# Two-layer linear attention and MLP on one core: the deferred queries' min(q, 0) on VectorE, and layer 0's tiles 6 and 7 turned by VectorE

## The chip, the cores and the metric

The kernel runs on one core of a Trainium2 chip, in one launch. The metric is the device time of that core in microseconds (us). Before the change it is 867.03 us, the median of 3 runs (866.54 to 867.05).

The engines of a core have one instruction stream each and run at the same time: TensorE (PE in the profile; its weight loads are listed apart as PEld), VectorE (DVE), ScalarE (ACT), GpSimd (POOL) and SyncE (SP). They wait for each other through semaphores. Within one engine the instructions run in the order in which they were written. Here SP issues nearly all DMA transfers, one after the other, and an issue whose data is not yet there holds all issues behind it.

## The reference

Two layers, each an attention block and then an MLP block, over x of 2048 rows by 448. Cut to what matters here:

```python
phi = lambda t: jnp.where(t > 0, t + 1, jnp.exp(t)) + 1e-6
pq, pk = phi(q), phi(k)                      # q, k, v from layernorm(x) @ wqkv, 16 heads of 28
kv = jnp.einsum("bhsd,bhse->bhde", pk, v)
z = jnp.einsum("bhsd->bhd", pk)
num = jnp.einsum("bhqd,bhde->bhqe", pq, kv)
den = jnp.einsum("bhqd,bhd->bhq", pq, z)[..., None] + 1e-6
x = x + (num / den).transpose(...).reshape(B, S, D) @ wo
x = x + gelu(layernorm(x) @ w1 + b1) @ w2 + b2
```

The kernel computes phi as max(t, 0) + exp(min(t, 0)), with the 1e-6 added elsewhere. Everything is in float32; each matmul operand is split into a high and a low part, and three products of these parts make up one float32 product.

## The kernel before

x is handled in 16 row tiles of 128 (0 to 15), four to a block. Each layer has three stages.

Phase 1 (`phase1`) makes, for each tile t, the keys K(t), the queries Q(t) of tiles up to 8, and G, the running sum of x'k that later gives kv; G of tile t - 1 follows K(t) on TensorE. For K and Q the normalised tile is needed transposed, as `XH` (high part) and `XL` (low part). There are two ways to get there. For tiles below `TURNED[l]` (8 in layer 0, 0 in layer 1) TensorE transposes four pieces into a PSUM bank `tp` (`stage_b`, line 264), and ScalarE and VectorE split the bank into XH and XL (lines 276 and 277); the 64-column tail of such a tile is first copied twice by ScalarE (line 446). For the others VectorE turns 32x32 blocks into a tile `sq` (`turn`, lines 303 and 304), SP stores two turned tiles together to DRAM (`store_sq`, line 310) and reads them back spread over the partitions in four transfers (`spread`, line 318), and ScalarE and VectorE split the spread tile `sp` (`split_t`, lines 335 and 336).

The order of the work in a step t of phase 1 is written out as a string of tokens, `STEP`, with exceptions in `STEPS`: K, G and Q are the products; T the TensorE transposes of tile t + 1; X the split of tile t + 1 into XH and XL; s the split of tile t for G; kp, kh and kl the key's phi and its parts; a and n the normalisation of a later tile (`a10` is tile 10), tu or v its turn, sp the spread; qp the previous query's phi and its store to DRAM; bg a piece of the weights' loading and splitting; ld a load of x. In a product, `k_at`, `q_at` and `g_at` say at which places the low parts stand among the high ones.

The last products of phase 1 and the transition to the MLP are ordered by the tokens of `ORDER`: Q, Qy and Qa are products of the deferred queries of tiles 9 to 15; T3 and x3 the TensorE transposes and split of the last tile of the first MLP block, sp0 and sp1 the spreads of its first three tiles (half of these eight transfers are issued by ScalarE), x0 to x2 their splits; Qi is `phi_first` (ScalarE's relu(-q) and exp of its negative, lines 579 and 580), Qj `phi_last` (VectorE's max and sum, line 585, and SP's store), pre four loads of stored queries. After the last token ScalarE loads the table for Gelu and the first MLP product `hp` is issued.

The MLP stage runs over four blocks of four tiles, with 14 column groups each: `mlp1` makes `hp` for one group ahead (11 matmuls), ScalarE its Gelu `g` and high part `gh` (lines 974 and 977), VectorE its low part `gl` (line 978), and `mlp2` the 12 matmuls into `y` (lines 1001 to 1003: gh by w2h, gh by w2l, gl by w2h, for four tiles).

Of the kernel before, what the change touches and what calls it, by code (L numbers as in the profile page):

```python
# [11 lines left out]
AF = mybir.ActivationFunctionType  # L12
OP = mybir.AluOpType
# [9 lines left out]
def linear_attn_mlp_kernel(  # L23
# [12 lines left out]
    pe, act, dve, pool, sp = nc.tensor, nc.scalar, nc.vector, nc.gpsimd, nc.sync  # L36
    x0 = x_in[0]
    y_out = out[0]
    S, D = x0.shape
    F = w1.shape[1]  # L40
    H, DH = 16, 28
    NT = S // 128
    NB = NT // 4
    NF = F // 128
    G = 112
# [27 lines left out]
    def t512(tag, bufs, name, dt=F32, at=0):  # L73
        n = 576 if tag in "BF" else 512
        return work.tile([128, n], dt, name=name, tag=tag, bufs=bufs)[:, at:at + 512]
# [339 lines left out]
    bg = bg_pieces()  # L415
# [14 lines left out]
    sts = {}  # L430


    TURNED = (8, 0)
    tails = {}

    def stage_a(l, t):
# [46 lines left out]

    def k_at(l, t):
        if t < 9:
            return (3, 6, 9, 11) if t == 0 or l == 0 and 2 < t < 8 else (2, 5, 8, 11)
        return (2, 5, 8, 11) if t == 9 else (1, 4, 7, 10)

    def q_at(l, t):
        if t < 9:  # L490
            return (2, 5, 8, 11) if l == 0 and t < 7 else (2, 4, 7, 10) if t == 0 else (1, 4, 7, 10)
        return {11: (4, 7, 10, 11), 12: (5, 7, 9, 11),
                13: (5, 8, 10, 11), 15: (1, 5, 8, 11)}.get(t, (1, 4, 7, 10))

    def g_at(l, t):
        if t < 9:
            return (4, 7, 10) if l == 0 and 0 < t < 6 else (3, 6, 9)
        return (2, 5, 8) if t < NT - 1 else (2, 6, 9)

    def stage_k(l, t, cs=range(4)):  # L500
# [44 lines left out]
    qo = []  # L545
# [3 lines left out]
    def stage_q(l, t, cs=range(4), tag=None):  # L549
        if tag:  # L550
            qs_[l, t] = bank(tag, 4, "psq")[:, :D]
        qs_[l, t] = proj("q", ("a", l, t // 4), t % 4, qs_.get((l, t)), cs, q_at(l, t))
        if 3 in cs:
            qo.append((l, t, qs_.pop((l, t))))
# [19 lines left out]
    begun = []  # L574

    def phi_first():
        l, t, o = qo.pop(0)
        e = t512("e" if t < NT - 2 else "E", 3 if t < NT - 2 else 2, "eq")[:, :D]
        act.activation(e, o, AF.Relu, scale=-1.0)
        act.activation(e, e, AF.Exp, scale=-1.0)  # L580
        begun.append((l, t, o, e))

    def phi_last():
        l, t, o, e = begun.pop(0)
        dve.scalar_tensor_tensor(e, o, 0.0, e, op0=OP.max, op1=OP.add)
        sp.dma_start(pq_d[l][t * 128:(t + 1) * 128, :], e)
# [21 lines left out]
    def stage_g(l, t, acc, mid=lambda: None):  # L608
# [22 lines left out]
    ORDER = [  # L631
# [4 lines left out]
    ] * LAYERS  # L636
    DEFER = NT - sum(tok in ("Q", "Qa", "Qy") for tok in ORDER[0].split())

# [1 line left out]
    STEPS = {  # L640
# [9 lines left out]
    }  # L650
    NORM = (
# [464 lines left out]
    for l in range(LAYERS):  # L1116
# [11 lines left out]
        def pre(j):  # L1128
# [4 lines left out]

        tok_ = SimpleNamespace(
            Q=lambda j: stage_q(l, fill.pop(0)), Qp=lambda j: fill_qphi(), Qv=lambda j: stage_qphi(j or 9),
            Qi=lambda j: phi_first(), Qj=lambda j: phi_last(), Qx=lambda j: stage_q(l, fill[0], (0,)),
            Qy=lambda j: stage_q(l, fill.pop(0), (1, 2, 3)),
            Qa=lambda j: stage_q(l, fill.pop(0), tag="acc"), G=lambda j: stage_g(l, NT - 1, acc, lambda: trans_z(tr, zs[l])),
            ld=lambda j: (load_pq(l, 0, j), load_x(l, j)), gt=lambda j: trans_gt(tr, acc),
# [77 lines left out]
```

## Time and profile before

| | |
|---|---|
| median of 3 runs | 867.03 us |
| the profiled execution | 866.77 us |
| its span, first to last instruction | 865.0 us |
| granted TensorE clock | 1.00 throughout |
| data moved by DMA | 95.81 MB, mean 111 GB/s |
| DVE, ACT and POOL busy | 57%, 41% and 24% of the span |

Times in the profile's rows are microseconds from the start of the span. A row of a timeline has the start, the duration, the engine, the line of the kernel, the operation, what it writes and reads, and in brackets the idle time before it with what ended it. TensorE pipelines its matmuls: a row's duration is longer than the distance to the next, so its rate is read from starts or from windows. SPq and ACTq are DMA issues. A window's row has its length, the busy time and count of each engine, the granted clock, the DMA engines' share and GB/s.

### The profile page before, as it was taken

Reading aid. Unit: us, or ns where it says so; the run is one execution under the profiler, and the core shown is the slowest. Engines: PE = TensorE matmul, PEld = TensorE weight load, DVE = VectorE, ACT = ScalarE, POOL = GpSimd, SP = SyncE. Lnnn points to the kernel's source line nnn. Section 1 sums busy time; section 2 is a strip of 40 time slices with the busy share of each in tenths; the row PEclk is TensorE's granted clock in tenths of the full one; section 3 lists DMA queues with packets and bytes.
Section 4 is the critical chain, followed back from the end, with each engine's and each line's share of the span. In section 5 each row is a group of like instructions: output and inputs, shape, how many; then the busy total and the mean of one; then the engine's idle time right before and its main releaser. Section 6 shows DMA issues by size and latency. Waiting matters only on the chain.

```text
span 865.0 us, 11671 instructions
## 1 busy us (share of the span) xinstructions
PE 859.5 (99%) x4173; PEld 769.9 (89%) x4173; DVE 489.9 (57%) x956; ACT 354.0 (41%) x634; POOL 209.1 (24%) x242
## 2 busy tenths in 40 slices
PE   9999999999999999999999999999999999999998
PEld 8999988888888888888899998988888888888887
DVE  7888676559455443236477877664674383533112
ACT  6776656333323322333356565632232233223231
POOL 3565612235013012012222343120220140140000
PEclk9999999999999999999999999999999999999999
DMA  5475546633313502051145543362332423111001
GB/s 168 131 241 178 187 112 206 194 112 109 135 60 114 150 0 98 1 182 49 49 149 187 164 129 97 108 217 81 116 107 91 135 74 114 50 49 42 1 1 43
DMA packets 65082, 95.81 MB, mean 111 GB/s; under 512 B 9088, under 2 KB 59904, under 8 KB 65024
## 3 DMA queue, kind: packets, MB, share of 16 engines
q1 hardware_dynamic: 63696, 94.13, 33.8%
q10 hardware_dynamic: 1328, 0.93, 0.4%
q8 instruction: 33, 0.54, 0.3%
q14 instruction: 25, 0.20, 0.1%
HBM read 56.70 MB, written 35.13 MB: 106 GB/s over the span
## 4 chain that ended last, share of the span: by engine, by line
PE 95%; ACT 2%; DMA 1%; DVE 1%; issue 0%; POOL 0%; ACTq 0%; SPq 0%; DVEq 0%
PE hp L972 31%; PE y L1002 10%; PE y L1001 10%; PE y L1003 10%; PE G L622 8%; PE psk L353 8%; PE psq L353 5%; PE op L891 2%; PE op L890 2%; PE op L892 2%; DMA sp<-sq_m 1%; PE op L880 1%; PE op L879 1%; PE op L881 1%; PE kvp L786 1%; PE mp L796 1%
## 5 line engine op out<-in xcount | busy, mean ns | idle before, releaser
L978 DVE TENSOR_TENSOR gl<-g,gh 128x512 fp32r<-128x512 f32 x112 | 83.2, 743 | 293.2 <-ACT gh L977 293.2
L974 ACT ACTIVATE g<-hp,b1s 128x512 f32<-128x512 f32 x112 | 77.1, 688 | 400.1 <-PE hp L972 400.1
L1002 PE MATMUL y<-w2l,gh 128*128 128x448 f32 x447 | 163.6, 366 | 0.0
L1001 PE MATMUL y<-w2h,gh 128*128 128x448 f32 x447 | 162.2, 363 | 0.0
L1003 PE MATMUL y<-w2h,gl 128*128 128x448 f32 x447 | 160.3, 359 | 0.1
L972 PE MATMUL hp<-XH,w1h 128*128 128x512 f32 x336 | 130.7, 389 | 0.0
L972 PE MATMUL hp<-XH,w1l 128*128 128x512 f32 x336 | 130.7, 389 | 0.0
L972 PE MATMUL hp<-XL,w1h 128*128 128x512 f32 x336 | 130.1, 389 | 0.0
L215 POOL TENSOR_TENSOR brs<-bve,mhalf 128x1 f32<-128x1 f32 x55 | 34.8, 632 | 258.4 <-DVE bve L214 257.9
L1001 PEld LDWEIGHTS y<-w2h,gh 128*128 128x128 f32 x447 | 83.7, 187 | 9.8 <-ACT gh L977 0.5
L1002 PEld LDWEIGHTS y<-w2l,gh 128*128 128x128 f32 x447 | 83.9, 188 | 6.9
L1003 PEld LDWEIGHTS y<-w2h,gl 128*128 128x128 f32 x447 | 84.0, 188 | 5.8 <-DVE gl L978 0.9
L972 PEld LDWEIGHTS hp<-XL,w1h 128*128 128x128 f32 x336 | 63.1, 188 | 13.1
L972 PEld LDWEIGHTS hp<-XH,w1h 128*128 128x128 f32 x336 | 63.0, 187 | 10.7
L972 PEld LDWEIGHTS hp<-XH,w1l 128*128 128x128 f32 x336 | 63.1, 188 | 9.9
L977 ACT CAST gh<-g 128x512 fp32r<-128x512 f32 x112 | 69.6, 622 | 3.6
L840 POOL TENSOR_TENSOR pz<-pq,zb 128x448 f32<-128x448 f32 x32 | 37.0, 1162 | 103.3 <-DVE dn L846 67.1
L353 PE MATMUL psk<-wk,XH 128*128 128x448 f32 x210 | 61.8, 364 | 0.0
L353 PE MATMUL psq<-wq,XH 128*128 128x448 f32 x196 | 57.5, 366 | 0.0
L478 POOL TENSOR_TENSOR xnl<-x,xnh 128x384 fp32r<-128x384 f32 x32 | 35.0, 1092 | 69.3 <-ACT xnh L477 56.0
L622 PE MATMUL G<-kh,xnh 128*128 128x448 f32 x128 | 46.8, 368 | 0.0
L336 DVE TENSOR_TENSOR XL<-sp,XH 128x512 fp32r<-128x512 f32 x54 | 45.3, 851 | 2.1 <-ACT XH L335 2.1
(185 smaller groups left out, 1491.1 us busy)
## 6 DMA issues: line engine op xcount, KB each, us to landing
x<-in_A_x_dram SPq DMA_DIRECT2D x32, 224.0 KB, 3.7
pq_d<-eq SPq DMA_DIRECT2D x32, 224.0 KB, 2.7
pq<-pq_d SPq DMA_DIRECT2D x32, 224.0 KB, 3.1
sq_m<-sq SPq DMA_DIRECT2D x14, 512.0 KB, 2.6
x<-x_d SPq DMA_DIRECT2D x32, 224.0 KB, 3.7
sp<-sq_m SPq DMA_DIRECT2D x52, 128.0 KB, 2.8
sq_a<-sq SPq DMA_DIRECT2D x12, 512.0 KB, 2.9
sp<-sq_a SPq DMA_DIRECT2D x48, 128.0 KB, 2.7
```

Source lines behind the costliest of these rows:

```text
L336: eng.tensor_tensor(lo.rearrange("p (c i n) -> p c i n", c=4, n=32), x, f(h), op=OP.subtract)
L353: pe.matmul(o, x, p, start=(i == 0), stop=(i == 10))
L478: pool.tensor_tensor(lo[:, :TL], xn[:, :TL], f(h[:, :TL]), op=OP.subtract)
L622: pe.matmul(acc[c], w, k, start=first and c not in others[0], stop=last and c not in others[1])
L840: pool.tensor_tensor(pz, pqt[l, b * 4 + j], tr.zb, op=OP.mult)
L972: pe.matmul(o, w, r, start=(k == 0), stop=(k == len(made) - 1))
L974: act.activation(g, hp, AF.Gelu_apprx_tanh, bias=b1s[:, i:i + 1])
L977: act.copy(gh, g)
L978: dve.tensor_sub(gl, g, f(gh))
L1001: pe.matmul(acc[j], gh[:, s], w2h[:, i], start=first, stop=False)
L1002: pe.matmul(acc[j], gh[:, s], w2l[:, i], start=False, stop=False)
L1003: pe.matmul(acc[j], gl[:, s], w2h[:, i], start=False, stop=stop)
```

## The change

It has two parts.

In layer 0, `TURNED` goes from 8 to 6: tiles 6 and 7 take the way over VectorE and DRAM. The steps 3 to 11 of layer 0 are written anew: tile 7's and 8's normalisation stand earlier, each turn from tile 9 on stands in the step after its normalisation, the split X stands in some steps behind or ahead of the key's phi, and the places of the low parts in the products change to fit.

In the transition of both layers, three of the five deferred queries of `ORDER`'s end get their min(q, 0) from VectorE (`phi_min`, token Qm) and only the exponential from ScalarE (`phi_exp`, token Qe), and the first query's pair of ScalarE instructions moves ahead of T3.

```diff
-    TURNED = (8, 0)
+    TURNED = (6, 0)
...
-            return (3, 6, 9, 11) if t == 0 or l == 0 and 2 < t < 8 else (2, 5, 8, 11)
+            return (3, 6, 9, 11) if t == 0 or l == 0 and 2 < t < 6 else (2, 5, 8, 11)
...
-            return (2, 5, 8, 11) if l == 0 and t < 7 else (2, 4, 7, 10) if t == 0 else (1, 4, 7, 10)
+            return (2, 5, 8, 11) if l == 0 and t < 5 else (2, 4, 7, 10) if t == 0 else (1, 4, 7, 10)
...
-            return (4, 7, 10) if l == 0 and 0 < t < 6 else (3, 6, 9)
+            return (4, 7, 10) if l == 0 and 0 < t < 4 else (3, 6, 9)
...
+    def phi_min():
+        l, t, o = qo.pop(0)
+        e = t512("e" if t < NT - 2 else "E", 3 if t < NT - 2 else 2, "eq")[:, :D]
+        dve.tensor_scalar(e, o, 0.0, None, op0=OP.min)
+        begun.append((l, t, o, e))
+
+    def phi_exp():
+        e = begun[-1][3]
+        act.activation(e, e, AF.Exp)
...
-        "o2 lb0 tu0 la2 o3 lb1 tu1 st0 la3 lb2 tu2 st1 Qy Q lb3 T3 sp0 sp1 Qi Qa x3 Qj x0 x1 x2 Qi Qj pre "
-        "Qa Qi Qj Qa Qi Qj Qi Qj "
+        "o2 lb0 tu0 la2 o3 lb1 tu1 st0 la3 lb2 tu2 st1 Qy Q Qi lb3 T3 sp0 Qm sp1 Qe Qj Qa Qj Qm x3 Qe "
+        "Qj x0 Qa Qm x1 x2 Qe Qj pre Qa Qi Qj "
...
-        (0, 3): "qp K T X s a7 kp kh n6 kl a8 G bg Q ld",
-        (0, 4): "qp K T X s a9 kp kh n7 n8 kl n9 v8 v9 G bg Q ld sp",
-        (0, 8): "qp K T X s a kp n kh kl tu a14 G bg Q ld sp",
-        (0, 9): "qp K T X s kp n14 kh kl v14 G bg",
-        (0, 10): "K T X s a15 kp n15 kh kl v15 G bg sp",
-        (0, 11): "K T X kp s kh kl G bg",
+        (0, 3): "qp K T X n6 s a7 kp kh n7 kl v6 v7 G bg Q ld sp",
+        (0, 4): "qp K T X s a8 kp kh n8 a9 kl v8 n9 G bg Q ld",
+        (0, 5): "qp K s kp X kh v9 a10 kl n10 G bg Q ld sp",
+        (0, 6): "qp K s X v10 kp kh a11 kl n11 G bg Q ld",
+        (0, 7): "qp K s v11 kp X kh a12 kl n12 G bg Q ld sp",
+        (0, 8): "qp K s v12 kp X kh a13 kl n13 a14 G bg Q ld",
+        (0, 9): "qp K X s v13 kp n14 kh kl G sp bg",
+        (0, 10): "K X s v14 kp a15 kh kl n15 G bg",
+        (0, 11): "K X v15 kp s kh kl G sp bg",
```

How it moves the instructions, at the three places of which the prediction speaks.

VectorE at the tail of layer 0's phase 1, before, from the key's low part in step 10 on (psk is the key's product, XL<-sp the split of the next tile):

```order
L442 TENSOR_SCALAR x_15_964<-x_15_964,bmv,brs 128x448
L526 SCALAR_TENSOR_TENSOR kl<-psk,kh 128x448
L533 TENSOR_TENSOR za<-psk,za 128x448
L303 STREAM_TRANSPOSE sq<-x_15_964 128x3x4x32
L304 STREAM_TRANSPOSE sq<-x_15_964 128x4x32
L336 TENSOR_TENSOR XL<-sp,XH 128x512
L372 SCALAR_TENSOR_TENSOR psk<-psk,ek 128x448
```

and in the change:

```order
L526 SCALAR_TENSOR_TENSOR kl<-psk,kh 128x448
L533 TENSOR_TENSOR za<-psk,za 128x448
L442 TENSOR_SCALAR x_15_960<-x_15_960,bmv,brs 128x448
L336 TENSOR_TENSOR XL<-sp,XH 128x512
L303 STREAM_TRANSPOSE sq<-x_15_960 128x3x4x32
L304 STREAM_TRANSPOSE sq<-x_15_960 128x4x32
L372 SCALAR_TENSOR_TENSOR psk<-psk,ek 128x448
```

Tile 15's turn, which stood ahead of the split of tile 12, now stands behind it; tile 13's turn moved behind the split of tile 10 in the same way.

SP at the same place, the store and the spread of tiles 14 and 15 before (L101, L103 and L104 are loads of weight pieces):

```order
L101 DMA stg<-in_B_w_dram 128x448
L310 DMA sq_a_3_1_1064<-sq 128x1024
L103 DMA stg<-in_B_w_dram 64x448
L104 DMA stg<-in_B_w_dram 64x448
L318 DMA sp<-sq_a_3_1_1064 32x4x256 x4
```

and in the change:

```order
L101 DMA stg<-in_B_w_dram 128x448
L103 DMA stg<-in_B_w_dram 64x448
L104 DMA stg<-in_B_w_dram 64x448
L310 DMA sq_a_3_1_1094<-sq 128x1024
L318 DMA sp<-sq_a_3_1_1094 32x4x256 x4
```

Two weight loads moved ahead of the store.

ScalarE at the transition of layer 0, from the copy of the last tile's tail to the first Gelu, before (eq is a query's phi, XH the splits):

```order
L918 COPY xm_3_1625<-xm_3_1625 128x64
L318 DMA sp<-sq_m_0_0_1589 32x4x256 x2
L318 DMA sp<-sq_m_0_1_1603 32x4x128 x2
L579 ACTIVATE eq<-psq 128x448
L580 ACTIVATE eq<-eq 128x448
L276 CAST XH<-tp 128x512
L335 CAST XH<-sp 128x512 x3
L579 ACTIVATE eq<-psq 128x448
L580 ACTIVATE eq<-eq 128x448
L579 ACTIVATE eq<-psq 128x448
L580 ACTIVATE eq<-eq 128x448
```

(two more such pairs follow, then the table load) and in the change:

```order
L579 ACTIVATE eq<-psq 128x448
L580 ACTIVATE eq<-eq 128x448
L931 COPY xm_3_1628<-xm_3_1628 128x64
L318 DMA sp<-sq_m_0_0_1589 32x4x256 x2
L318 DMA sp<-sq_m_0_1_1603 32x4x128 x2
L591 ACTIVATE eq<-eq 128x448
L276 CAST XH<-tp 128x512
L591 ACTIVATE eq<-eq 128x448
L335 CAST XH<-sp 128x512 x3
L591 ACTIVATE eq<-eq 128x448
L579 ACTIVATE eq<-psq 128x448
L580 ACTIVATE eq<-eq 128x448
```

The table load follows here directly; one pair is ahead of the copy, three exponentials stand alone, and one pair is left behind the splits instead of four.

More of the change, by code (lines that the diff above doesn't have):

```diff
@@ L1135, in linear_attn_mlp_kernel @@
             Q=lambda j: stage_q(l, fill.pop(0)), Qp=lambda j: fill_qphi(), Qv=lambda j: stage_qphi(j or 9),
-            Qi=lambda j: phi_first(), Qj=lambda j: phi_last(), Qx=lambda j: stage_q(l, fill[0], (0,)),
+            Qi=lambda j: phi_first(), Qm=lambda j: phi_min(), Qe=lambda j: phi_exp(), Qj=lambda j: phi_last(), Qx=lambda j: stage_q(l, fill[0], (0,)),
             Qy=lambda j: stage_q(l, fill.pop(0), (1, 2, 3)),
```

## The prediction, written before the change had run

> **What bounds the kernel now.** I read the page's busy shares first, then the chain that ended last, then who waited for whom on TensorE's weight loads.
>
> ```profile
> PE 859.5 (99%) x4173; PEld 769.9 (89%) x4173; DVE 489.9 (57%) x956; ACT 354.0 (41%) x634; POOL 209.1 (24%) x242
> ...
> PE 95%; ACT 2%; DMA 1%; DVE 1%; issue 0%; POOL 0%; ACTq 0%; SPq 0%; DVEq 0%
> ```
>
> ```profile
> PEld y L1003 <- DVE gl L978: 0.9, 2, 0.4
> PEld y L1001 <- ACT gh L977: 0.5, 2, 0.3
> ```
>
> TensorE is the bound: 859.5 of 865.0 us. A change gains only by taking instructions off TensorE or by ending one of its few waits. The second fence gives the waits that this change aims at: two places (one in each layer, at the first MLP block's first second-layer product), where the weight load waits 0.3 us for ScalarE's `gh` and then 0.4 us for VectorE's `gl`. All other engines have idle time, so work moved to them costs nothing unless it makes a tile late.
>
> **Part one, fewer transposes.** The chain of waits has four TensorE transposes ahead of G in the steps of tiles 5 and 6, and the windows compare two such steps with the next one, which has none.
>
> ```profile
> 42.98 0.44 PE tp L264 x4
> ...
> 50.03 0.44 PE tp L264 x4
> ```
>
> ```profile
> 40.77:47.82 7.05, 7.05 (x38) 6.58 (x38) 6.79 (x16) 4.73 (x10) 4.46 (x6) 1.00 0.44 149
> 47.82:54.87 7.05, 7.05 (x38) 6.58 (x38) 5.31 (x12) 4.98 (x10) 4.07 (x5) 1.00 0.83 257
> 54.87:61.48 6.61, 6.61 (x35) 6.18 (x34) 5.56 (x13) 5.21 (x11) 5.17 (x6) 1.00 0.73 237
> ```
>
> Each window is one step, and its first two columns are its length and TensorE's busy time. The steps with a transposition last 7.05 us, the one without 6.61: 0.44 each. Tiles 6 and 7 lose theirs, so this part takes 2 x 0.44 = 0.88 us off the path. ScalarE also loses two tail copies, which it had time for.
>
> What comes instead: VectorE turns the two tiles, SP issues one store of 512 KB and four spreads of 128 KB, and the splits read the spread tile in SBUF where they read a PSUM bank.
>
> ```profile
> 67.32 0.57 DVE L303 STREAM_TRANSPOSE sq<-x 128x384 f32<-128x384 f32 x1
> 67.81 0.27 DVE L304 STREAM_TRANSPOSE sq<-x 128x128 f32<-128x128 f32 x1
> 68.00 0.59 DVE L209 BATCH_NORM_STATS2 bst<-x 128x6 f32<-128x448 f32 x1
> ```
>
> A turn holds VectorE from 67.32 to 68.00: 0.68 us, two of them 1.36. VectorE (the fourth figure of each window) is 5.31 to 6.79 us busy in steps of 6.61 to 7.05, so this is the tightest of the covers, and what counts is whether a tile's pieces are there when TensorE loads them. I work out two places.
>
> ```profile
> L442 DVE TENSOR_SCALAR x<-x,bmv,brs 128x448 f32<-128x448 f32 x30 | 18.6, 624 | 6.4 <-POOL brs L215 5.6
> ```
>
> ```profile
> 35.03 0.62 DVE L209 BATCH_NORM_STATS2 bst<-x 128x6 f32<-128x448 f32 x1
> ...
> 36.14 0.62 DVE L372 SCALAR_TENSOR_TENSOR eq<-psq,eq 128x448 f32<-128x448 f32 x1
> ```
>
> ```profile
> 44.98 0.58 ACT L370 ACTIVATE ek<-ek 128x448 f32<-128x448 f32 x1
> ```
>
> ```profile
> 68.11 0.33 SPq L310 DMA_DIRECT2D sq_a<-sq  x1
> ...
> 71.03 1.75 SPq L318 DMA_DIRECT2D sp<-sq_a  x4
> ...
> 80.08 0.32 SPq L310 DMA_DIRECT2D sq_a<-sq  x1
> ...
> 83.03 1.76 SPq L318 DMA_DIRECT2D sp<-sq_a  x4
> ```
>
> ```profile
> 87.37 0.62 ACT L335 CAST XH<-sp 128x512 fp32r<-128x512 f32 x1 [0.88 <-DMA sp<-sq_a]
> ```
>
> ```profile
> 88.02 0.69 DVE L336 TENSOR_TENSOR XL<-sp,XH 128x512 fp32r<-128x512 f32 x1 [0.79 <-ACT XH L335]
> ```
>
> ```profile
> 89.77 0.19 PEld L353 LDWEIGHTS psk<-wk,XL 128*128 128x128 f32 x1
> ```
>
> The round trip through DRAM is read from the last four fences: store issued 80.08, spreads 2.95 later, ScalarE's cast of tile 14 starts 87.37 having waited for the spread. That is 7.29 us from store to cast and 1.34 more to the end of XL (88.71). TensorE loads it at 89.77, so tile 14 had 1.06 us to spare.
>
> First place, tiles 6 and 7. In step 3 VectorE starts tile 8's statistics at 35.03 and the next query's sum at 36.14. The change puts tile 7's normalisation (0.62) and the turns (1.36) here and moves the statistics behind: 36.14 - 1.11 + 0.62 + 1.36 = 37.0 for the store, and 7.29 later, 44.3, the earliest cast of tile 6. ScalarE comes to that cast only after the exponential of key tile 5, which ends at 45.56 now, so it hides the trip with 1.3 to spare. From 45.56, 1.34 for cast and subtraction give 46.9. Key tile 6 now starts at 47.82 and would at 47.4, loading its first XL about 0.2 ahead (for tile 14 the load is at 89.77 and the chain's product at 90.14): 0.3 to spare.
>
> Second place, the tail, which is tighter. Every tile from 10 on is turned one step later than now. Tile 13's turn now stands behind tile 10's subtraction, and tile 15's behind tile 12's (the order rows of layer 0's tail, ahead of this prediction).
>
> ```profile
> 69.91 1.50 DVE L336 TENSOR_TENSOR XL<-sp,XH 128x512 fp32r<-128x512 f32 x1
> ```
>
> ```profile
> L336 DVE TENSOR_TENSOR XL<-sp,XH x8: 651/1060/1495, 57.1 to 92.0; 128x512 fp32r<-128x512 f32 x8
> ```
>
> ```profile
> L277 DVE TENSOR_TENSOR XL<-tp,XH x6: 673/686/692, 17.9 to 51.1; 128x512 fp32r<-128x512 f32 x6
> ```
>
> Tile 10's subtraction starts at 69.91 now; 0.88 earlier is 69.03. It takes between 0.65 and 1.50, the turn 0.68: the store of tiles 12 and 13 goes out between 70.4 and 71.2 (now 68.11). Plus 7.29: cast of tile 12 at 77.7 to 78.5, its subtraction ends 1.34 later, turn of tile 15, store of 14 and 15 at 79.7 to 80.5. Plus 7.29 + 1.34: XL of tile 14 done between 88.3 and 89.1, wanted at 89.77 - 0.88 = 88.9. The margin is +0.6 to -0.2, where it was 1.06. I take a loss of 0.1 us here: most of the interval is safe, but two stage loads (L103, L104) now stand ahead of the last store on SP and wait for GpSimd.
>
> **Part two, the deferred queries.** Now ScalarE does relu and exponential for five queries, four of them behind the spread casts, then loads the Gelu table.
>
> ```profile
> 127.50 0.25 ACT L918 COPY xm<-xm 128x64 f32<-128x64 f32 x1 [1.21 <-DVE xm L227]
> ...
> 136.07 0.53 ACT L579 ACTIVATE eq<-psq 128x448 f32<-128x448 f32 x1
> 136.63 0.58 ACT L580 ACTIVATE eq<-eq 128x448 f32<-128x448 f32 x1
> 137.23 1.28 ACT L204 ACT_TABLE_LOAD   x1
> 138.52 0.20 ACT L204 ACTIVATE none<-tiny 128x1 f32<-128x1 f32 x1
> 138.63 0.67 ACT L974 ACTIVATE g<-hp,b1s 128x512 f32<-128x512 f32 x1
> 139.33 0.62 ACT L977 CAST gh<-g 128x512 fp32r<-128x512 f32 x1
> ```
>
> ```profile
> 135.01 0.39 PE L972 MATMUL hp<-XH,w1h 128*128 128x512 f32 x1
> ...
> 137.28 0.39 PE L972 MATMUL hp<-XL,w1x 128*128 128x512 f32 x1
> ```
>
> ```profile
> 131.04 0.69 DVE L277 TENSOR_TENSOR XL<-tp,XH 128x512 fp32r<-128x512 f32 x1 [3.57 <-ACT XH L276]
> ```
>
> In the change the first query's pair goes into ScalarE's idle 1.21 us ahead of the copy at 127.50. The three middle ones give their relu to VectorE (three minima, into its idle 3.57 us and the gaps after it). The last pair is then ready as soon as its product ends, at 135.01, where now it starts at 136.07. ScalarE starts the table load 1.0 us earlier, at 136.2, and `g` at 137.6; hp of that block has its last matmul at 137.28, so it is there. `gh` ends 138.9 (now 139.95) and `gl`, 0.69 like any such subtraction from 131.04, 139.6. TensorE wants `gh` at 139.7 (the product's start of 140.00 below less the 0.3 waited) and `gl` two loads later, 140.1: 0.8 and 0.5 to spare, so the stall ends. Its size:
>
> ```profile
> 140.00:142.84 2.84, 2.79 (x13) 1.00 0.99 340
> 145.34:147.74 2.40, 2.40 (x14) 1.00 0.48 150
> 565.34:568.18 2.84, 2.79 (x14) 1.00 1.01 371
> ```
>
> The stalled twelve matmuls last 2.84 in both layers, the next block's 2.40: 0.44 each, 0.88 together.
>
> A minimum from PSUM is not in the trace. From below I bound it by the 0.53 of ScalarE's relu on the same data, from above by the 0.62 of VectorE's sum L372, which reads the same PSUM tile and one tile more (fence of step 3). I take 0.6, the same engine's row. Three are 1.8 us for VectorE; if its cover were gone, a minimum late by more than 0.5 would bring the stall back. The four query stores ahead of the preloads of pq hold SP until the fourth sum; the preloads then start some 0.5 us later than now, and what reads them stands on VectorE behind `gl` of the second block, later than that.
>
> **The sum.** 0.88 + 0.88 - 0.1 = 1.66 us. The profiled execution took 866.77 us (span 865.0), 0.26 under the median of 867.03; its span would be 863.3. From the median: **865.4 us**.
>
> **Rivals.** First, a tile comes late by a little. Either both round trips of the tail are longer by some L: the first lateness delays the second store, so tile 14 is late by twice L less the margin, taken as 0.2 in the middle. For it speaks
>
> ```profile
> DMA to landing us min/median/max: 2.5/2.9/3.8
> ```
>
> for these spreads, 0.9 between median and maximum; against it, that the first leg took 2.92 and 2.95 us in the two trips shown. With L = 0.4 the loss is 0.6. Or tile 6's subtraction takes the longest time that the rows show from `sp`, 1.50 where 0.69 was counted: 0.8 more than counted, 0.3 of it spare, a loss of 0.5. Both give 865.9. The Trainium skill, SBUF — State Buffer, Who interferes with whom, says that a VectorE instruction with two SBUF inputs contends with a GpSimd one that reads SBUF, the later one blocking entirely, which speaks against reading tiles 6 and 7 from `sp`. By that rule, the trace agrees: 651 to 1495 ns from `sp`, 673 to 692 from the PSUM bank.
>
> Second, and on the other side: the DRAM trips become the path. The change adds a fifth trip to a stretch where DMA is 0.73 to 0.83 busy (last but one figure of the windows). If both legs of a trip go to 3.8 (L = 1.8), the tail loses 2 x 1.8 - 0.2 = 3.4, and tile 6 loses 1.8 - 1.3 - 0.3 = 0.2: 867.03 - 1.76 + 3.6 = 868.9. It decides from L = 1.0, where 1.8 us of loss in the tail eat the gain. The Trainium skill, VectorE: DVE Perf Modes, Rules for kernel authors, would not have made this change at all: it puts a 128x128 transposition on TensorE where PSUM will do as the destination. The trace has that choice at 0.44 us a tile on the engine that sets the end.
>
> Third, part two does not do what it says: the exponentials that wait for VectorE's minima hold ScalarE's casts and the last pair, and the stall stays. For it speaks that ScalarE runs in order and now waits for VectorE twice between the casts; against it the 0.5 us to spare. Then only part one is left, 867.03 - 0.88 + 0.1 = 866.3.
>
> **Chances.** The forecast (both parts, loss up to 0.3) 60%, first rival 20%, third 6%, second 14%. A measurement of this kernel tells about 0.2% (1.73 us) from no change, so faster means under 865.30. The clean sum without the 0.1 is 865.27, just beyond: I give half of the forecast's 60% to faster, 30%; the other half, the first and the third rival and a little of the second to no change, 58%; the rest, 12%, to slower. The likeliest case alone spans 865.1 to 865.7. The range reaches from 865.0 up to 867.4 and leaves out the slow end of the second rival and little below.
>
> **What would show it.** Steps of tiles 5 and 6 at 6.61 us; twelve matmuls in 2.40 at the start of both MLP stages, with the table load about 1.0 us earlier relative to the first hp. For the tail: TensorE's weight load of XL for key tile 12 or 14 waiting for VectorE, or the wait absent. A wait at key tile 6 would show VectorE too full; a wait for `gl` that remains would show part two wrong.

## The result and the profile after

The change takes 865.65 us, the median of 20 runs (865.01 to 867.07), against 866.93 for the kernel before (20 runs, 866.22 to 867.84): 1.28 us less, ratio 0.9987 with a 95% interval of 0.9981 to 0.9993. That is under the 0.2% that counted as a change in the prediction, and still a gain, since the interval lies below 1. The profiled execution has a span of 863.8 us at a granted clock of 1.00. One further execution of the change, among the eleven of run 8 below, took 2239.27 us at the same clock; no trace of it was kept, and the median given there leaves it out.

Lines of `kernel.py` behind `phi_exp` are 13 higher than before: `hp` is L985, `g` L987, `gh` L990, `gl` L991, `y` L1014 to L1016. The minimum is L586, the exponential alone L591, the query's sum L595.

The page of the changed kernel, its busy time and its chain of waits:

```profile
PE 858.9 (99%) x4165; PEld 770.2 (89%) x4165; DVE 494.4 (57%) x966; ACT 350.3 (41%) x626; POOL 209.8 (24%) x242
...
PE 98%; DMA 1%; DVE 0%; issue 0%; SPq 0%; ACT 0%; DVEq 0%; ACTq 0%
```

TensorE has eight instructions fewer, VectorE ten more (four for the two turns, six minima), ScalarE eight fewer. TensorE still sets the end.

The windows of three key tiles' steps (5, 6 and 7), each from the first matmul of a key's product to that of the next, and of the first twelve matmuls of `y` in both layers, from the first of them to the first `hp` behind them. The first column behind the window is its length, the next TensorE's busy time:

```profile
40.66:47.27 6.61, 6.61 (x34) 6.19 (x33) 4.72 (x12) 4.50 (x10) 4.15 (x5) 1.00 0.95 294
47.27:54.19 6.92, 6.90 (x34) 6.12 (x33) 6.85 (x15) 4.54 (x10) 4.65 (x5) 1.00 0.77 234
54.19:60.79 6.60, 6.60 (x34) 6.19 (x33) 6.46 (x15) 5.93 (x12) 4.83 (x6) 1.00 0.90 312
139.47:141.87 2.40, 2.40 (x14) 2.25 (x13) 0.83 (x2) 1.31 (x2) 0.85 (x1) 1.00 0.83 265
564.36:566.76 2.40, 2.40 (x14) 2.25 (x12) 0.83 (x2) 1.31 (x2) 0.92 (x1) 1.00 0.93 279
```

A step without transposes takes 6.61, and the twelve matmuls of `y` last 2.40 in both layers, so both parts did what they were to do. The step of key tile 6 is the exception, 6.92. Who made TensorE's weight loads wait says why; of the waits of before the two of `y` are gone, and one is new in the steps:

```profile
PEld psk L353 <- DVE XL L336: 0.4, 1, 0.4
```

The launch ahead of the first G matmul took between 16.65 and 17.54 us in the profiled executions below, with the same code. So I compare executions by the time from the first G matmul to the end of the last `y`: before 844.56 us (17.04 to 861.60), after 843.10 (17.09 to 860.18), 1.46 less. The two parts should give 1.76; the 0.3 that is missing is key tile 6's.

### The profile page after: what moved, and what is told of

Its sections match the earlier page's. It is cut to its first block, busy times and chain, and to the rows that moved or that the text cites. A ratio compares the mean times of both kernels' runs of the same rounds, so it can differ in the third digit from the quotient of the medians.

```text
span 863.8 us, 11682 instructions
## 1 busy us (share of the span) xinstructions
PE 858.9 (99%) x4165; PEld 770.2 (89%) x4165; DVE 494.4 (57%) x966; ACT 350.3 (41%) x626; POOL 209.8 (24%) x242
## 4 chain that ended last, share of the span: by engine, by line
PE 98%; DMA 1%; DVE 0%; issue 0%; SPq 0%; ACT 0%; DVEq 0%; ACTq 0%
PE hp L985 32%; PE y L1015 10%; PE y L1014 10%; PE y L1016 10%; PE G L632 8%; PE psk L353 8%; PE psq L353 7%; PE op L904 2%; PE op L903 2%; PE op L905 2%; PE op L893 1%; PE op L892 1%; PE op L894 1%; PE kvp L799 1%; PE mp L809 1%; PE psk L567 1%
## 5 line engine op out<-in xcount | busy, mean ns | idle before, releaser
L991 DVE TENSOR_TENSOR gl<-g,gh 128x512 fp32r<-128x512 f32 x112 | 83.2, 743 | 293.8 <-ACT gh L990 293.8
L987 ACT ACTIVATE g<-hp,b1s 128x512 f32<-128x512 f32 x112 | 77.1, 688 | 400.8 <-PE hp L985 400.8
L1014 PE MATMUL y<-w2h,gh 128*128 128x448 f32 x447 | 162.0, 362 | 0.0
L1016 PE MATMUL y<-w2h,gl 128*128 128x448 f32 x447 | 160.0, 358 | 0.0
L985 PE MATMUL hp<-XH,w1h 128*128 128x512 f32 x336 | 130.7, 389 | 0.0
L985 PE MATMUL hp<-XH,w1l 128*128 128x512 f32 x336 | 130.7, 389 | 0.0
L985 PE MATMUL hp<-XL,w1h 128*128 128x512 f32 x336 | 130.1, 389 | 0.0
L1014 PEld LDWEIGHTS y<-w2h,gh 128*128 128x128 f32 x447 | 83.7, 187 | 9.4
L1016 PEld LDWEIGHTS y<-w2h,gl 128*128 128x128 f32 x447 | 84.0, 188 | 5.0
L985 PEld LDWEIGHTS hp<-XL,w1h 128*128 128x128 f32 x336 | 63.1, 188 | 13.1
L985 PEld LDWEIGHTS hp<-XH,w1h 128*128 128x128 f32 x336 | 63.0, 187 | 10.7
L985 PEld LDWEIGHTS hp<-XH,w1l 128*128 128x128 f32 x336 | 63.1, 188 | 9.9
L990 ACT CAST gh<-g 128x512 fp32r<-128x512 f32 x112 | 69.6, 622 | 3.6
```

The source lines that it names most:

```text
L985: pe.matmul(o, w, r, start=(k == 0), stop=(k == len(made) - 1))
L987: act.activation(g, hp, AF.Gelu_apprx_tanh, bias=b1s[:, i:i + 1])
L990: act.copy(gh, g)
L991: dve.tensor_sub(gl, g, f(gh))
L1014: pe.matmul(acc[j], gh[:, s], w2h[:, i], start=first, stop=False)
L1016: pe.matmul(acc[j], gl[:, s], w2h[:, i], start=False, stop=stop)
```

## Where key tile 6 was late

ScalarE in the changed kernel, from the key's high part in step 4 to the cast of tile 6:

```profile
40.15 0.64 ACT L517 ACTIVATE kh<-psk,tiny 128x448 fp32r<-128x448 f32 x1 [1.17 <-DVE psk L372]
41.40 0.57 ACT L403 CAST w1x<-stg 128x448 fp32r<-128x448 f32 x1 [0.61 <-DMA stg<-in_B_w_dram]
43.21 0.57 ACT L400 CAST w1h<-stg 128x448 fp32r<-128x448 f32 x1 [1.24 <-DMA stg<-in_B_w_dram]
...
45.76 0.58 ACT L370 ACTIVATE ek<-ek 128x448 f32<-128x448 f32 x1
46.25 0.60 ACT L335 CAST XH<-sp 128x512 fp32r<-128x512 f32 x1
```

The cast of tile 6 waits for no transfer. It stands behind `ek`, and all of this is late because ScalarE waited 0.61 and 1.24 us for two weight pieces (`stg`). SP shows why they were late, first in the kernel before, then in the change:

```profile
31.58 0.47 SPq L103 DMA_DIRECT2D stg<-in_B_w_dram  x1
32.10 0.60 SPq L104 DMA_DIRECT2D stg<-in_B_w_dram  x1
32.80 0.53 SPq L101 DMA_DIRECT2D stg<-in_B_w_dram  x1
```

```profile
37.56 0.33 SPq L310 DMA_DIRECT2D sq_a<-sq  x1
37.94 0.47 SPq L103 DMA_DIRECT2D stg<-in_B_w_dram  x1
38.46 0.65 SPq L104 DMA_DIRECT2D stg<-in_B_w_dram  x1
39.21 0.56 SPq L101 DMA_DIRECT2D stg<-in_B_w_dram  x1
39.88 0.38 SPq L85 DMA_DIRECT2D x<-in_A_x_dram  x1
40.53 1.77 SPq L318 DMA_DIRECT2D sp<-sq_a  x4
```

In step 3 the change writes the turns (`v6 v7`) ahead of `bg`. The store waits for VectorE's second turn, and SP holds the three loads behind it until 37.94, 6.4 us later than before. My theory was then: 0.88 for the transposes, 0.88 for the two stalls of `y`, and 0.28 lost because these loads hold up ScalarE.

That theory leaves out a second way in which the loads delay tile 6. The four spreads, the last of them issued at 41.87, took this long from issue to landing:

```profile
DMA to landing us min/median/max: 4.2/4.2/4.2
```

So the spread was there at 46.1, 8.5 us behind its store, and only 0.2 us ahead of the cast at 46.25. A ScalarE that had waited for no weight piece could have started the cast hardly earlier; by an estimate from these rows (cast from 46.15, 0.1 earlier) the longer trip by itself would have kept 0.2 of the 0.3 us lost. Runs 3 and 6 bear on this.

## The experiments

Each run was timed beside the kernel before on the same chip: runs 1 to 4 on one chip, 5 to 8 on a second, 9 to 11 on a third, with eleven executions each (four of run 5). The ratio is estimated from the single executions; it is not the quotient of the two medians. "G to end" is the time from the first G matmul to the end of the last `y` in the profiled execution.

| run | median us | before | difference | ratio, 95% interval | G to end, against 844.56 |
|---|---|---|---|---|---|
| the change | 865.65 | 866.93 | -1.28 | 0.9987 (0.9981 to 0.9993) | -1.46 |
| 1 part two alone | 865.96 | 866.16 | -0.20 | 0.9996 (0.9987 to 1.0004) | -0.66 |
| 2 part one alone | 865.82 | 866.16 | -0.34 | 1.0003 (0.9995 to 1.0012) | -1.06 |
| 3 loads ahead | 865.02 | 866.16 | -1.14 | 0.9988 (0.9979 to 0.9997) | -1.34 |
| 4 new order, no minima | 865.31 | 866.16 | -0.85 | 0.9993 (0.9984 to 1.0002) | +0.48 |
| 5 minima, old order | 874.53 | 866.62 | +7.91 | 1.0092 (1.0077 to 1.0108) | +7.42 |
| 6 casts behind | 865.27 | 866.62 | -1.35 | 0.9986 (0.9977 to 0.9994) | -1.26 |
| 7 preloads ahead | 865.18 | 866.62 | -1.44 | 0.9984 (0.9975 to 0.9993) | -1.63 |
| 8 the change again | 865.64 | 866.62 | -0.98 | 0.9989 (0.9980 to 0.9998) | -0.66 |
| 9 both fixes | 865.05 | 866.65 | -1.60 | 0.9981 (0.9972 to 0.9990) | -1.76 |
| 10 both fixes, no minima | 865.02 | 866.65 | -1.63 | 0.9979 (0.9970 to 0.9988) | -1.80 |
| 11 loads ahead again | 865.26 | 866.65 | -1.39 | 0.9984 (0.9975 to 0.9992) | -1.81 |

### 1 and 2: each part alone

Run 1 is the kernel before with `phi_min`, `phi_exp` and the new `ORDER`; run 2 is the change with the old end of `ORDER`:

```diff
-        "o2 lb0 tu0 la2 o3 lb1 tu1 st0 la3 lb2 tu2 st1 Qy Q Qi lb3 T3 sp0 Qm sp1 Qe Qj Qa Qj Qm x3 Qe "
-        "Qj x0 Qa Qm x1 x2 Qe Qj pre Qa Qi Qj "
+        "o2 lb0 tu0 la2 o3 lb1 tu1 st0 la3 lb2 tu2 st1 Qy Q lb3 T3 sp0 sp1 Qi Qa x3 Qj x0 x1 x2 Qi Qj pre "
+        "Qa Qi Qj Qa Qi Qj Qi Qj "
```

> Part two alone: layer 0 turns tiles 8 to 15 as in the kernel before, and only the deferred queries get the new order and the three minima. Theory (the change is two independent gains less one new stall): 0.44 us less in each layer, 0.88 us under the kernel before; no TensorE weight load of y waits for gh or gl; twelve matmuls in 2.40 us in both layers; no wait for XL at key tile 6. Rival (the two parts help each other, for instance because part one gives ScalarE or VectorE time in the transition): less than 0.6 us, and a wait of the first y stays.

> Part one alone: tiles 6 and 7 turned by VectorE, the deferred queries as in the kernel before. Theory: 0.88 us of transposes gone, 0.28 lost at key tile 6, so 0.60 us under the kernel before; the weight load of XL at key tile 6 waits about 0.4 us, and both waits of y (0.5 for gh, 0.9 for gl, two of each) are back. Rival (the moved turns also slow the transition or the tail): less than 0.4 us gained, or a wait of XL at key tile 12 or 14.

In run 2 the waits of `y` came back (0.8 for `gl`, 0.3 for `gh`), as expected, but key tile 6 did not wait at all in its profiled execution: ScalarE's second wait for a weight piece was 0.41 us there instead of 1.24. That execution gained the whole 0.88 of part one (G to end -1.06, since one of the two waits for `gh` was absent too). Its runs fall in two groups: seven between 865.33 and 865.88, four between 867.35 and 868.18 (they lift its ratio above 1). No trace of the longer group was kept here; run 4 below has one, and its loss is at tile 6.

In run 1 the waits of `y` did not go entirely; one for `gl` stayed in each layer:

```profile
PEld y L1013 <- DVE gl L988: 0.3, 2, 0.2
```

`gl` took 1.14 and 1.18 us instead of 0.69 there. I had not expected that; runs 3, 4, 6 and 8 explain it. Neither part alone is a gain clear of noise by the times (both intervals hold 1); that each works is read from the waits and steps of the traces.

### 3: the stage loads ahead of the store

```diff
-        (0, 3): "qp K T X n6 s a7 kp kh n7 kl v6 v7 G bg Q ld sp",
+        (0, 3): "qp K T X n6 s a7 kp kh n7 kl G bg v6 v7 Q ld sp",
```

> The changed kernel with one edit in the step of tile 3: the stage loads of w1 are issued on SP ahead of the turns' store, where in the change they stand behind it and go out at 37.94 us (in the kernel before at 31.58). Theory (key tile 6 is late because ScalarE, in order, waits 0.61 and 1.24 us for those loads ahead of its cast XH of tile 6): the loads go out at about 31.6 again, both waits of ScalarE end, the cast of tile 6 starts by 45.6 instead of 46.25, XL ends by 47.0 instead of 47.60, the wait at key tile 6 is gone and the time falls by 0.25 to 0.3 us against the change, to 1.76 under the kernel before less what other waits take. Rival A (the spread's trip through DRAM is what is late): the cast then waits for the spread and TensorE's wait stays near 0.4. Rival B (VectorE is too full in this stretch): the cast comes earlier, but the subtraction still ends at 47.6 and the wait stays.

SP and ScalarE in run 3:

```profile
31.32 0.47 SPq L103 DMA_DIRECT2D stg<-in_B_w_dram  x1
...
37.24 0.33 SPq L310 DMA_DIRECT2D sq_a<-sq  x1
```

```profile
40.36 0.56 ACT L403 CAST w1x<-stg 128x448 fp32r<-128x448 f32 x1
40.82 0.57 ACT L400 CAST w1h<-stg 128x448 fp32r<-128x448 f32 x1
...
44.77 0.62 ACT L335 CAST XH<-sp 128x512 fp32r<-128x512 f32 x1 [0.82 <-DMA sp<-sq_a]
```

The loads go out at 31.32, both waits are gone, the cast of tile 6 starts 1.48 us earlier (1.16 against the first G matmul, which came 0.32 earlier here) and now waits for the spread alone, 7.53 us behind its store. The spreads landed sooner too:

```profile
DMA to landing us min/median/max: 2.6/2.8/3.1
```

XL ended at 46.16 and TensorE did not wait for it. Tile 6 is in time, as the theory said, and rival B fell, since VectorE's work is as it was. But the edit took away two delays at once, ScalarE's waits and the slower spreads, so this run doesn't decide between the theory and rival A. The 0.3 came back, but 0.44 went elsewhere: in layer 1 `y` waited for `gl` again. VectorE and GpSimd there:

```profile
562.70 1.15 POOL L853 TENSOR_TENSOR pz<-pq,zb 128x448 f32<-128x448 f32 x1 [12.06 <-DMA pq<-pq_d]
562.86 1.53 DVE L991 TENSOR_TENSOR gl<-g,gh 128x512 fp32r<-128x512 f32 x1 [2.12 <-ACT gh L990]
```

GpSimd's product `pz` starts when the first preload of stored queries lands. Here that was 0.16 us ahead of `gl`, and `gl` took 1.53: it ended 0.54 behind the end of `pz`.

### 4 and 5: which half of part two does the work

Run 4 keeps the new order and gives the three relus back to ScalarE; run 5 keeps the minima and takes the old order:

```diff
+        "o2 lb0 tu0 la2 o3 lb1 tu1 st0 la3 lb2 tu2 st1 Qy Q Qi lb3 T3 sp0 sp1 Qi Qj Qa Qj x3 Qi "
+        "Qj x0 Qa x1 x2 Qi Qj pre Qa Qi Qj "
```

```diff
+        "o2 lb0 tu0 la2 o3 lb1 tu1 st0 la3 lb2 tu2 st1 Qy Q lb3 T3 sp0 sp1 Qi Qa x3 Qj x0 x1 x2 Qm Qe Qj pre "
+        "Qa Qm Qe Qj Qa Qm Qe Qj Qi Qj "
```

> The changed kernel with its new order of the deferred queries, but without the minima: the three middle queries do relu and exponential on ScalarE again, at the place where the change has the exponential alone. Theory (moving the first pair ahead and taking three relus off ScalarE both bring the table load forward, and the second is what clears the casts): ScalarE has 3 x 0.55 = 1.65 us more between 127.5 and 135; its gaps there take most of it, so the table load comes between 0.2 and 1.2 us later than in the change (135.85), and the wait of y comes back in part: 0 to 0.44 us lost in each layer, 0.4 in all as my middle. Rival (the order alone does it, the minima are not needed): no wait of y, the same time as the change within 0.1 us. Other rival (the minima alone do it): the full 0.88 us is lost.

> The counterpart of the run without minima: the changed kernel with the deferred queries in the order of the kernel before, the three last queries but one with minimum on VectorE and exponential alone on ScalarE. Theory after that run (there the order alone brought the table load 1.0 us forward against the step and the minima added nothing): the last query's pair again stands behind other queries' work, the table load comes at most 0.55 us earlier relative to the first hp than in the kernel before, and a wait for gl of 0.1 to 0.4 us stays in each layer; so 0.2 to 0.8 us longer than the change. Rival (either part suffices, since three relus fewer take 1.65 us off ScalarE): no wait of y, and the time of the change within 0.2 us.

The last pair and the table load, in the change and then in run 4:

```profile
134.68 0.55 ACT L579 ACTIVATE eq<-psq 128x448 f32<-128x448 f32 x1 [0.79 <-PE psq L353]
135.25 0.58 ACT L580 ACTIVATE eq<-eq 128x448 f32<-128x448 f32 x1
135.85 1.28 ACT L204 ACT_TABLE_LOAD   x1
```

```profile
135.69 0.55 ACT L579 ACTIVATE eq<-psq 128x448 f32<-128x448 f32 x1 [0.47 <-PE psq L353]
136.26 0.58 ACT L580 ACTIVATE eq<-eq 128x448 f32<-128x448 f32 x1
136.86 1.28 ACT L204 ACT_TABLE_LOAD   x1
```

In both the last pair waits for its own product on TensorE, by 0.79 and 0.47 us. Run 4's rows are 1.01 us later because all of TensorE is (below). The minima shorten ScalarE's queue, and that time is then spent waiting. My theory for run 4 was wrong, its first rival right in this: the order alone brings the table load forward. A wait for `gl` did occur in layer 1 (0.6 us), with `gl` at 1.60 beside `pz`; run 10 repeats the test without that.

Run 5 was much worse than either text expected. ScalarE in its transition:

```profile
133.62 0.58 ACT L591 ACTIVATE eq<-eq 128x448 f32<-128x448 f32 x1 [1.61 <-DVE eq L586]
135.43 0.58 ACT L591 ACTIVATE eq<-eq 128x448 f32<-128x448 f32 x1 [1.22 <-DVE eq L586]
137.22 0.58 ACT L591 ACTIVATE eq<-eq 128x448 f32<-128x448 f32 x1 [1.22 <-DVE eq L586]
137.71 0.53 ACT L579 ACTIVATE eq<-psq 128x448 f32<-128x448 f32 x1
...
138.87 1.28 ACT L204 ACT_TABLE_LOAD   x1
```

A minimum that stands behind the previous query's sum makes a chain across two engines: minimum, exponential, sum, next minimum, 1.8 us a query (133.62, 135.43, 137.22), with ScalarE idle 1.22 of them. In run 5 the whole chain stands behind the splits. The change has the same chain (its last two minima also stand behind the sum ahead), but its first minimum starts at 127.59 instead of 132.98, and the splits stand between its links, so ScalarE has casts to do and idles 0.94 and 0.27 us ahead of the second and third of these exponentials. Run 2 differs from run 5 by the minima alone: in the old order they turn a G to end of -1.06 into +7.42.

The first `y` was 2.65 us later behind the first `hp` than in the change, in each layer, and TensorE paid a second time; its windows in layer 0, where the column behind GpSimd's count is the granted clock:

```profile
134.00:138.70 4.70, 4.70 (x22) 3.91 (x21) 2.93 (x5) 2.23 (x5) 0.20 (x1) 1.00 0.58 170
138.70:141.60 2.90, 0.45 (x2) 0.03 (x1) 0.62 (x1) 2.84 (x6) 0.94 (x1) 1.00 0.84 223
141.60:145.20 3.60, 3.56 (x10) 2.84 (x11) 2.93 (x6) 1.19 (x2) 1.04 (x1) 0.54 0.97 359
145.20:148.00 2.80, 2.80 (x14) 2.41 (x13) 1.35 (x3) 0.00 (x0) 0.10 (x1) 0.98 0.63 201
```

In the second window TensorE worked for 0.45 of 2.90 us. Then its clock was 0.54 on average for 3.6 us, and ten matmuls took the time of some eighteen.

Run 4's profiled execution was one of its long ones (867.05 us; seven of its eleven lie under 865.6). It shows what happens at key tile 6 then:

```profile
45.00 0.58 ACT L370 ACTIVATE ek<-ek 128x448 f32<-128x448 f32 x1
46.70 0.62 ACT L335 CAST XH<-sp 128x512 fp32r<-128x512 f32 x1 [1.13 <-DMA sp<-sq_a]
```

Here ScalarE was free and the spread itself was late: its store was issued at 37.13, so the trip took 9.57 us where run 3 took 7.53. TensorE lost some 1.1 us at key tile 6. After it, from 50 to 79 us, each of its matmuls took 3 to 6 ns longer (202 to 209 against 196 to 205), 0.6 us together. Run 8 shows the same slow stretch without a large stall, so the stall isn't its cause, and the cause stays open.

### 6: two ways in which late loads can hurt

```diff
-        (0, 4): "qp K T X s a8 kp kh n8 a9 kl v8 n9 G bg Q ld",
-        (0, 5): "qp K s kp X kh v9 a10 kl n10 G bg Q ld sp",
+        (0, 4): "qp K T X s a8 kp kh n8 a9 kl v8 n9 G Q ld",
+        (0, 5): "qp K s kp X kh bg v9 a10 kl n10 G bg Q ld sp",
```

> The changed kernel with the stage loads still behind the turns' store on SP, but ScalarE's casts of them (and the issue of the next two loads) moved from the step of tile 4 to the step of tile 5, behind the cast XH of tile 6. It parts the two ways in which the late loads can hurt. Theory A (ScalarE's in-order wait for the loads is the whole of it): the cast of tile 6 starts at about 44.8 as in the run with the loads ahead, TensorE's wait at key tile 6 is gone, and the times scatter little. Theory B (the three loads also stand in the DMA queues directly ahead of the spreads and make the trip from store to landing longer, 9.57 us in the run without minima against 7.53 with the loads ahead): the cast itself waits for the spread and starts between 45.5 and 46.7, the wait at key tile 6 stays between 0.1 and 0.9 us, and some executions take over 1 us longer than the others, as in the run of part one alone.

ScalarE's cast of tile 6 in run 6:

```profile
45.52 0.62 ACT L335 CAST XH<-sp 128x512 fp32r<-128x512 f32 x1 [1.49 <-DMA sp<-sq_a]
```

With ScalarE free of the loads' casts, the cast of tile 6 waited for the spread, 8.14 us behind its store (37.38). That is 0.6 longer than in run 3, as theory B says, and still in time, as theory A says: tile 6 did not wait. The times lie between 864.85 and 866.17, without a second group.

So both ways are real, and the landings tell them apart. From the store's issue to the landing of the last spread of tiles 6 and 7 it took 7.2 to 7.5 us in the five runs with the loads ahead (3, 7, 9, 10 and 11), and 7.9 to 9.5 in the six with them in between (the change and runs 2, 4, 5, 6 and 8). In the change (8.5) and in run 4 (9.5) the spread was late by itself. In run 8 it was there at 45.4 and ScalarE came to the cast at 45.77, so there ScalarE's waits alone cost the 0.1 that was lost. Run 6 took 8.1; with the 8.5 of the change its tile 6 would have been late as well, by an estimate from the same rows.

### 8: the change again

> The change itself, on the same chip and beside the same runs of the kernel before as the other three. Theory: its times scatter over about 2 us, since the stall at key tile 6 and the first gl beside pz come out differently from one execution to the next; median 0.9 to 1.4 us under the kernel before; gl of the first block between 0.69 and 1.6 in the profiled execution, key tile 6 losing 0.2 to 1.0 us. Rival (the profiled execution shown first was typical): 0.28 lost at key tile 6 and gl at 0.69 in both layers again.

Its median is 0.98 under the kernel before. In the profiled execution key tile 6 lost 0.1, less than the theory's 0.2 to 1.0; `gl` took 0.99 and 1.50 us, `y` lost 0.4 in layer 1, and the slow stretch of run 4 cost some 0.6; so it is -0.66 where the first was -1.46. The first execution had been lucky; there `gl` came first, by 0.23 us:

```profile
138.61 0.69 DVE L991 TENSOR_TENSOR gl<-g,gh 128x512 fp32r<-128x512 f32 x1 [2.12 <-ACT gh L990]
...
138.84 1.48 POOL L853 TENSOR_TENSOR pz<-pq,zb 128x448 f32<-128x448 f32 x1 [12.46 <-DMA pq<-pq_d]
```

Whichever starts first keeps its time (0.69 or 1.15 us) and the other waits: `gl` behind `pz` ends 0.54 to 0.56 us after it, whatever its own start, and `pz` behind `gl` takes 1.48 here. The Trainium skill, SBUF — State Buffer, Who interferes with whom, says that a VectorE instruction with two SBUF inputs and a GpSimd one that reads SBUF contend for a shared read interface, and that the one issued first holds it for the whole instruction. By that rule, the trace agrees: in runs 1, 3, 4, 6 and 8 `gl` behind `pz` took between 0.96 and 1.69.

### 7, 9, 10 and 11: out of the collision

Run 7 is run 3 with `pre` moved up behind sp1; run 9 has it one place later, behind the first query's Qj; run 10 is run 9 without the minima; run 11 is run 3 again. Of run 9:

```diff
-        (0, 3): "qp K T X n6 s a7 kp kh n7 kl v6 v7 G bg Q ld sp",
+        (0, 3): "qp K T X n6 s a7 kp kh n7 kl G bg v6 v7 Q ld sp",
...
-        "... Qi lb3 T3 sp0 Qm sp1 Qe Qj Qa Qj Qm x3 Qe "
-        "Qj x0 Qa Qm x1 x2 Qe Qj pre Qa Qi Qj "
+        "... Qi lb3 T3 sp0 Qm sp1 Qe Qj pre Qa Qj Qm x3 Qe "
+        "Qj x0 Qa Qm x1 x2 Qe Qj Qa Qi Qj "
```

> The stage loads ahead of the store as before, and in both layers the four preloads of pq for the second block issued right behind the spreads of xm, ahead of the deferred queries' stores, so that GpSimd's first product pz (which waits for the first of them) is done before VectorE's first subtraction gl. Theory (gl takes 0.69 us alone and 0.96 to 1.60 beside pz, whose start the preload's landing sets; in the run with the loads ahead this brought the stall of 0.44 us back in layer 1): pz runs before 136 and 562, gl takes 0.69 in both layers, no wait of y in either, 0.44 us less than the run with the loads ahead, about 1.8 to 2.0 us under the kernel before, with the change between. Rival A (gl is slow for another reason): gl stays above 0.9 in a layer. Rival B (the preloads, now in the queues beside the spreads of xm, make a tile of the MLP late): a wait of hp for XH or XL, 0.2 us or more lost.

> The change with the stage loads ahead of the turns' store, and the four preloads of pq issued one place later than in the run with the preloads ahead: behind the first deferred query's store and ahead of the other four. Theory (the first g there waited 0.41 us in layer 0 for the buffer of a query whose store stood behind the preloads; that query's store is now ahead of them): pz still runs before 136 and 562, gl takes 0.69 in both layers, no wait of y and none of g for pq_d, no wait for XL at key tile 6. That leaves the whole 1.76 us of the two parts: 1.6 to 1.9 under the kernel before, 0.1 to 0.2 less than the run with the preloads ahead. Rival: g waits for another buffer or the stores of the other queries, and the 0.1 us stays.

> The same as the run with both fixes, but the three middle queries do relu and exponential on ScalarE: the change's new order without its minima. Theory (the first pair in ScalarE's idle gap and the last pair alone at the end carry the gain, the minima nothing): table load as early against the step, no wait of y, the same time as the run with both fixes within 0.2 us. Rival (the minima are needed, and the run without them was only hidden by its other waits): the first gh or gl late in a layer, 0.2 to 0.9 us longer.

> The run with the loads ahead once more, beside the two runs with the preloads moved. Theory (the first gl and pz collide by chance of the landing): gl takes 0.69 to 1.6 us in the two layers, a stall of up to 0.44 us in one or both, so 0.1 to 0.6 us longer than the run with both fixes; key tile 6 has no wait, and none of its executions is over 1.5 us above the fastest. Rival: the collision of the first run was an accident of that chip, gl is 0.69 in both layers, and it is as fast as the run with both fixes.

In run 7 `pz` was out of the way, but the first `g` of layer 0 waited 0.41 us for its buffer (`g <- DMA pq_d<-eq`), whose query's store now stood behind the preloads; some 0.1 of it reached TensorE. By median run 7 is 1.44 under the kernel before, short of the 1.8 to 2.0 that its theory gave. Run 9 mends the wait of `g`. GpSimd's first `pz` and VectorE's `gl` in both layers of run 9:

```profile
133.78 1.55 POOL L853 TENSOR_TENSOR pz<-pq,zb 128x448 f32<-128x448 f32 x1 [7.56 <-DMA pq<-pq_d]
...
558.48 1.16 POOL L853 TENSOR_TENSOR pz<-pq,zb 128x448 f32<-128x448 f32 x1 [7.36 <-DMA pq<-pq_d]
```

```profile
138.45 0.69 DVE L991 TENSOR_TENSOR gl<-g,gh 128x512 fp32r<-128x512 f32 x1 [2.12 <-ACT gh L990]
...
563.36 0.69 DVE L991 TENSOR_TENSOR gl<-g,gh 128x512 fp32r<-128x512 f32 x1 [2.11 <-ACT gh L990]
```

No wait of `y`, none at key tile 6, and G to end is 1.76 us under the kernel before: the whole of both parts. By median it is 1.60 under it. Run 10 does the same without a single minimum, 1.63 under. Run 11 shows what chance leaves to run 3: its profiled execution had `gl` at 0.69 in both layers (`gl` came 0.32 and 0.39 us ahead of `pz`) and -1.81, but its median stays at -1.39. The same kernel as run 3 gave -1.14 and the change itself -1.28 and -0.98 on different chips, so I don't put the 0.2 us between runs 9 and 11 down to the collision alone; the traces show that it can cost 0.4 to 0.6 a layer (runs 3, 4, 6 and 8), not how often. The change was not timed beside runs 9 and 10, and the intervals overlap: that the two fixes end the waits is shown by the traces, that they gain time over the change is not shown by the times.

## Why the prediction was right, and where it was off

The forecast was 865.4 us, or 1.66 under the kernel before; measured are 865.65, and 1.28 under it. Of the two terms of gain both stood, and the term of loss was mis-sized and put in the wrong place. That the total came within 0.3 us is in part luck: the loss counted in the tail did not come, and losses of the same order came at two places that the forecast held to be safe.

- **Fewer transposes, 0.88.** Right: steps of 6.61 and 6.60, and 0.88 in the executions in which tile 6 was in time (run 2).
- **The stall of `y`, 0.88.** Right in size (2.40 in both layers; the `hp` behind them 0.44 us earlier against the first `hp` in both) and through the step named, the table load that comes earlier. It came 0.85 us earlier against the first `hp` instead of 1.0: the last pair starts 0.20 behind that `hp` (134.68 for 134.48), when its product has ended, where the prediction took the start of `hp` for the end of the product. `gl` ended at 139.30 and was loaded at 139.67, 0.4 to spare for the 0.5 predicted. The minimum took 0.62, the upper bound; 0.6 was taken. But the three minima are not what does it. "The three middle ones give their relu to VectorE" stands in the prediction as a part of what ends the stall; run 10 has the whole gain without them, and in run 4 the table load comes as early. What works is the order: the first pair in ScalarE's idle gap and the last pair alone. No run parts these two.
- **The tail, a loss of 0.1.** It did not come. Every interval of that step held; ScalarE's casts of tiles 12 and 14 and what followed, in the change:

```profile
77.74 0.62 ACT L335 CAST XH<-sp 128x512 fp32r<-128x512 f32 x1 [0.61 <-DMA sp<-sq_a]
...
87.61 0.62 ACT L335 CAST XH<-sp 128x512 fp32r<-128x512 f32 x1 [1.65 <-DMA sp<-sq_a]
```

  The second store was issued at 80.25, so the trip took 7.36 (7.29 were taken); XL of tile 14 ended at 88.95 and was wanted at 89.24, 0.29 to spare. The 0.3 lost at tile 6 had put off that moment; in run 9, without that loss, it was 0.15 (88.93 and 89.08).
- **Tile 6, "0.3 to spare".** This is the step that failed. The store went out at 37.56 (37.0 predicted) and VectorE's subtraction took 0.68, so VectorE was not wrong by much. Two terms failed, for one reason: the step moves the store ahead of three loads on SP. In "from 45.56, 1.34 for cast and subtraction" the end of `ek` was read from the trace of before, as if nothing ahead of it on ScalarE moved; but ScalarE casts the data of these loads ahead of `eq` and `ek`, and `ek` ended at 46.34 instead of 45.56. And in "7.29 later" the trip was read in the tail, where two loads of 112 KB stand between the store and the spreads; here these three (448 KB) and one of x (224 KB) do, and it took 8.5 to the landing, to 46.1 instead of 44.3 for the earliest cast. Either one makes tile 6 late. The prediction looked for loads ahead of a store in the tail, not for a store ahead of loads here.
- **The preloads of pq.** "What reads them stands on VectorE behind `gl` of the second block" was wrong: GpSimd's `pz` reads them first and waits for nothing but the landing. Against the first `hp`, which starts 0.53 us earlier (134.48 for 135.01), the table load came 0.85 us earlier and the preloads, issued at 135.41 for 135.15, 0.8 later. In the kernel before `pz` started 1.9 to 2.0 us ahead of `gl` and was done; in the change and in runs 1, 3, 4, 6, 8 and 11 the two start within 0.75 us of each other.
- **The rivals.** The first had the right place in its second half (tile 6; 0.5 for the 0.3 measured) with another mechanism, a long subtraction; the contention that it named struck `gl` instead. The second, the DRAM trip as the path, does occur, at tile 6 and not in the tail: 8.5 us in the change, 9.57 in run 4's execution, with spreads that took 4.2 us where it reckoned with up to 3.8. The third did not. "A wait at key tile 6 would show VectorE too full" was a wrong reading in advance: run 3 took the wait away and left VectorE's work as it was.

## What to carry to other kernels

Before an instruction that waits is put ahead of others in an in-order queue, list what the queue holds behind it and who reads that: here a store on SP cost nothing itself, and the loads behind it reached TensorE in two ways, through ScalarE, which waited for them, and through the spreads that landed later behind them. When a wait can have two causes, look at when the data landed and not only at what the engine did last. When a stall is shortened, look at which instructions of the other engines now start beside it. And take a change apart before keeping it: of part two the order gave everything, and the minima in the old order made it 7.9 us slower than the kernel before.

## What was not expected of the hardware

- TensorE idle for some 2.45 us (2.90 less 0.45, run 5, layer 0) lost its clock: 0.54 on average for the 3.6 us that followed. In layer 1, after the same wait, it was 0.64 for 3.6 us and 0.86 for the next 2.9. The stalls of `y` in the kernel before, 0.4 us, leave it at 1.00. The Trainium skill, TensorE: Matmul & The Clock Gate, What's actually happening, says that the array falls to half rate after an idle window of about 3.4 us and needs one busy window of that length to come back. The trace agrees on the way back; here a shorter idle time was enough.
- Three weight loads (448 KB) issued between the store of tiles 6 and 7 and the spreads that read it back made the spreads land later: 7.2 to 7.5 us behind the store's issue without them (runs 3, 7, 9, 10 and 11), 7.9 to 9.5 with them (the change and runs 2, 4, 5, 6 and 8). Two smaller ones (224 KB together) in the tail of the kernel before left the trip to the cast at 7.29; in the tail of the change, without any, it took 6.89 and 7.36.
- In two profiled executions (runs 4 and 8) matmuls took 3 to 6 ns more from about 50 to 79 us at a granted clock of 1.00. The cause stays open.
